# Attention segments turned by VectorE in 32x32 blocks, and the output projection as four 128x32 quarters

## The chip, the cores and the metric

The kernel runs on one core of a Trainium2 chip. A core has TensorE (matrix products into PSUM, an accumulator memory of eight banks of 512 fp32 columns on 128 partitions), VectorE, ScalarE, GpSimd (the Pool) and SyncE, which issues DMAs. The profile calls them PE, DVE, ACT, POOL and SP, and TensorE's loads of the stationary operand PEld. The metric is the device time of one execution in microseconds.

## The reference

Four layers run one after the other on a sequence of 2048 positions of 512 features, each added to its input after a layer normalisation without weights:

```python
# layers 0 and 2: 32 query heads of 16, one key head and one value head for all
q = (x @ wq) as 32 heads;  k = x @ wk;  v = x @ wv
p = softmax(q . k * 16 ** -0.5)            # 2048 x 2048 for each head
x = x + (p @ v, heads side by side) @ wo
# layers 1 and 3: linear attention with phi(t) = (t + 1 if t > 0 else exp(t)) + 1e-6
kv = phi(k)^T v for each head;  z = sum of phi(k)
x = x + (phi(q) kv / (phi(q) z + 1e-6)) @ wo2
```

The inputs are bf16. Nearly all the work is in the softmax of layers 0 and 2: 2 x 32 x 2048 x 2048 scores, each with an exponential.

## The kernel before, in words

**Tiles.** The sequence is cut into 16 tiles of 128 positions. The queries of a tile are stored as 128 partitions by 512 columns: partition 32 j + 16 r + d, column 128 g + position, for head (g, j, r) and feature d. One score block is the product of 128 keys with four heads of one query tile: rows 32 j to 32 j + 31 of the array, 512 columns. The keys are stored twice, each time with half of the 32 rows masked to zero (`KM`, `kmask`), so that parity r = 0 or 1 selects a head of the pair. Two layers have 2 x 16 tiles x 2 parities x 16 key tiles x 4 = 4096 blocks.

**Segments.** All blocks of one query tile and one parity make a segment (`Seg`), 64 blocks (64 segments in both layers together). The value products of a segment (`pv_try`, L1213) add into one PSUM bank, `ACC`: group j writes partitions 32 j to 32 j + 31, of which 16 are the output, one is the sum of the exponentials and the rest are zero. Four groups run side by side in the array. A few segments at the start of a layer (four in layer 0, eight in layer 2) are done in pieces, as keys become ready, and their pieces are added up in SBUF (`sg.unit`, L1523 and L1525).

**Who takes the exponentials.** Two sets of three banks take turns. TensorE fills a set in one round of score products (`qk`, L1159). ScalarE does two, sometimes three, of the blocks of a set with one instruction (L1350). VectorE may take the third (`dve_split`) or one in a spare bank (`dve_open`): it writes the bits of an approximate power of two as an int16 (L1454); GpSimd makes three shifted copies of it with integer adds (L1496), and the four are used with four weighted values. A block of ScalarE needs one value product, one of VectorE four. Which engine takes a block is decided while the program is built, by thresholds on VectorE's and the buffers' backlog.

**The order of work.** The program's order is planned ahead: `Planner` goes through the program in time with the durations written beside each operation, and gives every engine a fixed list. Smaller `prio` goes first; `Pool_` objects hand out banks and buffers. A mode is kept with each TensorE operation: `row` for scores, `col` for value products, `full` for the others; a change of mode costs time in the plan. `TABLE` sets thresholds of the planner (such as `BLS`, `BLT`, `SPX` on VectorE's backlog, `FBS`, `LOW` on free buffers, `HMAX`, `HTOL`, `STICK` on TensorE's order) by planned time in microseconds. During the attention stretches nearly all banks belong to the two sets; bank 7 serves everything else, projections and statistics of the neighbouring layers included.

**The end of a segment.** `norms` copies the accumulator to SBUF as fp32 (L1523). `norm` then turns it with four 128x128 fp32 products with an identity (L1610) into a bank, takes the reciprocal of the sums (L1620) and multiplies (L1624) into `Osb`, now positions by features. When both parities of a tile are there, `epilogue` transposes `Osb` into `OT`, by a DMA for tiles below 12 and by TensorE above, multiplies with `wo` in four 128x128x512 products (`mm`, L844), and adds to `x_sb` (L1664). The last tile of each attention layer has versions of its own that work in halves, so that one half runs while the other waits (`norm_halves`, `epi_crit`).

**Setup.** Masks and the bf16 identity are made on VectorE and the Pool from a ramp and its transpose before the first tile (L774 to L789), `wo` is loaded in eight DMAs (L753).

Of the kernel before, what the change touches and what calls it, by code (L numbers as in the profile page):

```python
# [11 lines left out]
ALU = mybir.AluOpType  # L12
# [24 lines left out]
class Planner:  # L37
# [50 lines left out]
    def op(self, opts, reads=(), writes=(), prio=5.0, lat=0.08, dma=False, name="", join=None, mode="full", port=False, after=(), over=()):  # L88

        if not self.calm and any(k[0] == "bank" and k[1] == 7 for k in list(writes) + list(reads) if type(k) is tuple):  # L90
# [4 lines left out]
            if PE in opts and prio > DPP and self.ws(("bank", 7)) and all(x.eng != PE or not x.done for x in self.ws(("bank", 7))) and mode == "full":  # L95
                prio = DPP + 0.001 * prio
# [324 lines left out]
class Seg:  # L421
# [11 lines left out]
    def take(self, js, back=False):  # L433
# [61 lines left out]
       2: ONE, 3: [[0, 1], [2, 3], [4, 5], [6, 7], [8, 9], [10, 11], [12, 13]] + ONE[14:]}  # L495
# [26 lines left out]
PVE = 0.6  # L522
PHP = 5.9
# [36 lines left out]
    (5, dict(EVP=2.2, FBS=8, HTOL=0.12)),  # L560
    (180, dict(BLS=2.3, DPP=1.0, EVP=2.2, FBS=8, HTOL=0.12)),
    (210, dict(BLS=2.3, DPP=1.0, EVP=2.2, FBS=8, HMAX=0.35, HTOL=0.12, LOW=10)),
    (630, dict(BLS=2.3, BLX=2.4, DPP=1.0, EVP=1.2, FBS=8, HMAX=0.35, HTOL=0.12, LOW=10, OWNP=1.0, STICK=1.5)),
    (660, dict(BLS=2.3, BLT=3.4, BLX=2.4, DPP=1.0, EVP=1.2, FBS=8, HMAX=0.1, HTOL=0.12, LOW=10, OWNP=1.0, SPX=1.5, STICK=1.5)),
    (690, dict()),
    (720, dict(BLT=2.9, BLX=1.25, CHT=19, LOW=10)),
    (750, dict(BLT=2.9, BLX=1.25, CHT=19, LOW=10, OWNP=1.0, SPX=1.5)),
]
BASE = dict(BLS=BLS, BLT=BLT, BLX=BLX, CHT=CHT, DPP=DPP, EVP=EVP, FBS=FBS, HMAX=HMAX, HTOL=HTOL, LOW=LOW, OWNP=OWNP, SPX=SPX, STICK=STICK)


def bass_interleave_layers__grouped_kv_mqa__linear_attn_block__prompt_kernel(
# [33 lines left out]
    WO = [("wo", c, gl) for c in range(4) for gl in range(2)]  # L606
# [15 lines left out]
    rampT = sb("rampT", [P, 32], FP32)  # L622
    eps1 = sb("eps1", [1, H], BF16)
# [105 lines left out]
    def B_(i):  # L729
        return ("bank", i)  # L730
# [16 lines left out]
    def late():  # L747
        yield ("flag", ("K", 0, T - 1))
        pool_op(lambda e: e.memset(va[:].rearrange("p t (h c) -> p (t h) c", c=17)[:, :, DH:DH + 1], 1.0), [("va", i) for i in range(8)], dur=1.2, prio=5.0)
        wov = A_wo.rearrange("(gh gl j r d) c -> r gh gl j d c", gh=2, gl=2, j=4, r=2)  # L750
        for c in range(4):
            for gl in range(2):
                dma(wo[64 * gl:64 * gl + 64, c, :], wov[c // 2, c % 2, gl], [("wo", c, gl)], 3.0, 3.5)  # L753
# [19 lines left out]
    pool_op(lambda e: e.memset(ident[:], 0.0), ["ident"])  # L773
# [6 lines left out]
    for j in range(4):  # L780
        q_ = slice(32 * j, 32 * j + 32)
        o = op({DV: (0.1, lambda e, q_=q_: e.tensor_tensor(out=ident[q_, q_], in0=ramp[q_, :], in1=rampT[q_, :], op=ALU.is_equal))},
               reads=["ramp", "rampT"], writes=["ident"], prio=-4.0, lat=0.12, join=o)
# [1383 lines left out]
```

## Time and profile before

| what | us |
|---|---|
| median of three runs | 1362.88 |
| lowest and highest | 1362.84, 1363.64 |
| the profiled execution | 1362.91 |
| its span, first to last instruction | 1361.2 |
| first and last exponential of the attention layers (L1350) start at | 11.4 and 1325.4 |

The span is 1.7 us shorter than the time of the same execution, which also holds what lies before the first and after the last instruction. A line of a group gives line of the source, engine, operation, tiles written and read, shapes and count, then after the bar the time in which at least one of them ran, the mean length of one in ns, and after the second bar the time that the engine stood idle before them, with what ended it. Records of one engine can overlap, so a count times the mean can exceed the busy time. A line of a timeline gives start and length in us, the engine, the line and how many instructions are merged.

### The profile page before, as it was taken

The page shows a single profiled execution, that of the slowest core. Times are in us where ns is not written, and L with a number is a line of the kernel's source. Part 1 is how long each engine was busy: PE and PEld are TensorE (multiplying, and loading weights), DVE is VectorE, ACT ScalarE, POOL GpSimd, SP SyncE. Part 2 cuts the span into 40 slices and gives each one's busy share as a digit, 9 for nine tenths or more (in the row PEclk, how much of TensorE's full clock was granted, in tenths as well). Part 3 has the DMA queues.
Part 4 walks back from the last instruction along what each step waited for, and adds up shares of the span by engine and source line. Part 5 has one row for each costly group of instructions (what it writes and reads, how often), then busy time and mean ns, then how long its engine had stood idle before and what let it go on. Part 6 is the DMA issues. An engine that isn't in the chain of part 4 may idle for free.

```text
span 1361.2 us, 38320 instructions
## 1 busy us (share of the span) xinstructions
PE 1316.0 (97%) x14984; PEld 460.5 (34%) x15067; DVE 1216.7 (89%) x2195; ACT 1328.3 (98%) x1536; POOL 1054.8 (77%) x1063
## 2 busy tenths in 40 slices
PE   8999999999999999999999999999999999999998
PEld 4322323223333223223743323333332323233235
DVE  8899898999989999997879998889998899998987
ACT  7999999999999999999799999999999999999996
POOL 1699798989989898987005897768898798988980
PEclk9999999999999999999999999999999999999999
DMA  4300000000000000000022000000000000000001
GB/s 106 98 6 13 6 9 9 6 13 2 13 6 14 5 6 6 2 2 2 2 43 44 9 6 17 13 6 6 13 3 13 6 13 6 6 6 2 2 2 63
DMA packets 52482, 20.59 MB, mean 15 GB/s; under 512 B 46160, under 2 KB 51792, under 8 KB 52304
## 3 DMA queue, kind: packets, MB, share of 16 engines
q1 hardware_dynamic: 51248, 18.10, 6.2%
q8 instruction: 122, 2.00, 0.6%
q14 instruction: 56, 0.46, 0.1%
q10 hardware_dynamic: 1056, 0.03, 0.0%
HBM read 5.28 MB, written 2.10 MB: 5 GB/s over the span
## 4 chain that ended last, share of the span: by engine, by line
PE 54%; ACT 30%; issue 8%; DVE 6%; POOL 2%; DMA 0%; SPq 0%; ACTq 0%; POOLq 0%; DVEq 0%
ACT W L1350 28%; PE ps L1213 22%; PE ps L1159 17%; PE ps L844 6%; PE ps L1038 3%; DVE W L1454 3%; POOL W L1496 2%; PE ps L1610 2%; PE ps L1260 2%; ACT phE L1694 1%; DVE sacc L1523 0%; DVE xn L767 0%; DMA W<-xn 0%; PE ps L897 0%; ACT ve L927 0%
## 5 line engine op out<-in xcount | busy, mean ns | idle before, releaser
L1350 ACT ACTIVATE W<-ps 128x1024 bf16<-128x1024 f32 (+1 forms) x1330 | 1273.2, 1146 | 2.4 <-PE ps L1159 2.1
L1496 POOL INT64_ADD W<-W x1023 | 1047.9, 1036 | 268.9 <-DVE W L1454 124.6
L1454 DVE TENSOR_SCALAR W<-ps 128x512 int16<-128x512 f32 x1362 | 889.7, 684 | 89.7 <-PE ps L1159 72.8
L1213 PE MATMUL ps<-W,VV 128*32 128x512 bf16 x8182 | 616.8, 384 | 4.2 <-DVE sacc L1523 3.5
L1159 PE MATMUL ps<-W,KM 32*128 32x512 bf16 x4096 | 520.5, 385 | 18.7 <-ACT W L1350 12.7
L1159 PEld LDWEIGHTS ps<-W,KM 32*128 32x128 bf16 x4096 | 130.1, 91 | 496.8 <-ACT W L1350 441.4
L1213 PEld LDWEIGHTS ps<-W,VV 128*32 128x32 bf16 x8182 | 148.9, 94 | 251.4 <-issue 162.2
L844 PE MATMUL ps<-wqkv,W 128*128 128x512 bf16 (+1 forms) x230 | 66.6, 368 | 7.5 <-issue 5.1
L1694 ACT ACTIVATE phE<-ps 128x512 bf16<-128x512 f32 (+1 forms) x66 | 44.6, 677 | 3.9 <-PE ps L1038 2.6
L1260 PE MATMUL ps<-W,V 128*32 128x512 bf16 (+4 forms) x173 | 46.4, 340 | 0.4 <-DVE KM L1026 0.3
L1610 PE MATMUL ps<-identF,sacc 128*128 128x128 f32 x240 | 41.8, 289 | 0.0
L1523 DVE COPY sacc<-ps 128x512 f32<-128x512 f32 x60 | 40.8, 680 | 1.0 <-PE ps L1213 0.8
L938 DVE BATCH_NORM_STATS2 st<-x_sb 128x6 f32<-128x512 bf16 x60 | 40.5, 680 | 0.3
L1038 PE MATMUL ps<-W,wqkv 128*128 128x128 bf16 x512 | 39.4, 220 | 0.3 <-DVE W L1701 0.3
L1038 PE MATMUL ps<-W,wq 128*128 128x128 bf16 x464 | 35.8, 220 | 0.0
L844 PE MATMUL ps<-wo,OT 128*128 128x512 bf16 x90 | 29.4, 383 | 4.8 <-issue 3.3
L1038 PEld LDWEIGHTS ps<-W,wqkv 128*128 128x128 bf16 x512 | 30.2, 98 | 9.0 <-issue 5.7
L767 DVE TENSOR_SCALAR phE<-phE 128x513 bf16<-128x513 bf16 x50 | 21.2, 424 | 13.4 <-ACT phE L1694 12.3
L1610 PEld LDWEIGHTS ps<-identF,sacc 128*128 128x128 f32 x240 | 25.5, 141 | 16.1 <-issue 10.6
L1038 PEld LDWEIGHTS ps<-W,wq 128*128 128x128 bf16 x464 | 26.3, 98 | 12.3 <-issue 9.2
L844 PEld LDWEIGHTS ps<-wqkv,W 128*128 128x128 bf16 x272 | 18.3, 97 | 30.6 <-issue 19.1
L767 DVE TENSOR_SCALAR xn<-x_sb,mv,rs 128x513 bf16<-128x513 bf16 x52 | 27.1, 530 | 0.3 <-ACT rs L929 0.2
(156 smaller groups left out, 550.0 us busy)
## 6 DMA issues: line engine op xcount, KB each, us to landing
out_dram<-x_sb SPq DMA_DIRECT2D x16, 128.0 KB, 1.7
x_sb<-in_A_x_dram SPq DMA_DIRECT2D x6, 256.0 KB, 4.7
wqkv<-in_B_wqkv_dram SPq DMA_DIRECT2D x1, 1536.0 KB, 8.8
W<-xn SPq DMA_TRANSPOSE x46, 2.5
x_sb<-in_A_x_dram SPq DMA_DIRECT2D x4, 128.0 KB
wq<-in_A_wq_dram SPq DMA_DIRECT2D x1, 512.0 KB
wo<-in_A_wo_dram SPq DMA_DIRECT2D x8, 64.0 KB
wo<-in_B_wo_dram SPq DMA_DIRECT2D x1, 512.0 KB, 9.7
```

The source lines that it names most:

```text
L767: return e.add_instruction(mybir.InstTensorScalarPtr(name=nc.get_next_instruction_name(), engine=mybir.EngineType.DVE, op0=op0, op1=op1, i ...
L844: return e.matmul(dst, lhsT=l, rhs=r, start=(k == 0), stop=(k == len(pairs) - 1))
L1038: ins = e.matmul(dst[:, g * P:(g + 1) * P], lhsT=lhs(g, k), rhs=rhs(k), start=(k == 0), stop=(k == FT - 1))
L1159: return e.matmul(bank(b), lhsT=KM[r, sg.par, kt * P:(kt + 1) * P], rhs=QT[r, sg.t, :], start=True, stop=True)
L1213: ins = e.matmul(ps[32 * j:32 * j + 32, ACC * 512:(ACC + 1) * 512], lhsT=VV[:, kt, 0 if w is None else 1 + w, :], rhs=ap, start=(k == 0), ...
L1260: o = op({PE: (n / 2400.0, lambda e: e.matmul(ps[32 * j:32 * j + 32, b * 512:b * 512 + n], lhsT=V0[:], rhs=QT[:, sg.t, 0:n], start=st, sto ...
L1350: ex = op({AC: (EXO + 0.4267 * n, lambda e, n=n, s_=s_, p_=p_: e.activation(ws_(p_), ps[:, s_ * 512:(s_ + n) * 512], ACTF.Exp, scale=EXPSC ...
L1454: o = op({DV: (0.602, lambda e: e.tensor_scalar(out=dst.bitcast(I16), in0=bank(b), scalar1=VB, scalar2=VLO, op0=ALU.add, op1=ALU.max))}, w ...
L1496: o = op({PO: (512 * m * PSR + PSO, lambda e, g_=g_, f_=f_: e.int64_add(ws_(g_).bitcast(I64), ws_(f_).bitcast(I64), step))}, reads=wk_(f_) ...
L1523: o = op({DV: (0.6, lambda e, src=src: e.tensor_copy(src, bank(ACC)))}, writes=[B_(ACC)] + key, prio=0.0, lat=0.15)
L1610: o = op({PE: (0.12, lambda e, c=c: e.transpose(ps[:, b * 512 + c * P:b * 512 + (c + 1) * P], src[:, c * P:(c + 1) * P], identF[:]))}, rea ...
L1694: op({AC: (0.07 + n / 1200.0, lambda e: e.activation(phE[:, i, 0:n], bank(b, n), ACTF.Exp))}, reads=[B_(b)], writes=[("phE", i)], prio=pr ...
```

## The change

The accumulator is no longer copied and turned by TensorE. VectorE reads it with its own transpose, which turns each 32x32 block in place within the 128x512 tile: what was at partition 32 j + i, column 128 c + 32 b + a comes to partition 32 j + a, column 128 c + 32 b + i. Positions are now split: the partition holds the head group j and the position's low five bits a, the columns hold the position's block b. Reciprocal and multiply follow from SBUF, with the reciprocals in a PSUM bank taken for that only. For segments done in pieces the transpose comes after the last addition, as an instruction of its own from SBUF to SBUF.

`Osb` gets columns in the order b, c, r, d, so that a 128x128 transpose of its block b gives c, r, d on partitions and j, a in columns. The output projection therefore sums over j, and for each j has four products of 128x32 (one for each b), each writing 32 partitions of the result: `quarters`, in the mode `col`. `wo` is loaded in the matching order in four DMAs. The versions in halves for the last tile go away: that tile takes the common way, then two half transposes and a projection in two halves of 256 columns, in quarters too.

In the setup the masks come from two comparisons, the identity from one comparison and one multiply after the first tile's mean, and the memsets for the shifted values stand later in the Pool's queue. In layer 2, the normalisation of tiles 8 to 15 goes in pairs. `TABLE` has new rows, 16 for 8, and sets two more parameters (`AHEAD`, `DXB`); a threshold on the priority of products into bank 7 now holds for the mode `col` as well.

```diff
+TRD = 0.625
+    def quarters(e, b, cs, l, r, start, stop):
+        ins = None
+        for q in range(4):
+            ins = e.matmul(ps[32 * q:32 * q + 32, b * 512 + cs.start:b * 512 + cs.stop], lhsT=l[:, q, :], rhs=r, start=start, stop=stop)
+        return ins
...
                 if sg.first and sg.last:
                     a_ = yield ("acq", as_pool, 0.0)
                     src, key = acc_(a_)
+                    o = op({DV: (TRD, lambda e, src=src: e.transpose(src, bank(ACC)))}, writes=[B_(ACC)] + key, prio=0.0, lat=0.15)
                 else:
                     a_, (src, key) = None, acc_(sg.unit)
-                if sg.t in ECRIT and sg.par:
...
-        def norm_halves(sg, src, key, a_):
...
-        def epi_crit(t, k, m, pr):
...
         def norm(sg, src, key, a_):
...
+            if a_ is None:
+                raw, was = src, key
+                yield from until(*was)
+                a_ = yield ("acq", as_pool, pr)
+                src, key = acc_(a_)
+                op({DV: (TRD, lambda e: e.transpose(src, raw))}, reads=was, writes=key, prio=pr, lat=0.15)
...
-            for c in range(4):
-                o = op({PE: (0.12, lambda e, c=c: e.transpose(ps[:, b * 512 + c * P:b * 512 + (c + 1) * P], src[:, c * P:(c + 1) * P], identF[:]))},
-                       reads=key + ["identF"], writes=[B_(b)], prio=pr, lat=0.2)
...
-            v4 = bank(b).rearrange("p (c j d) -> p c j d", c=4, j=4)
-            rr = rden[:, r_, :].rearrange("p (c j) -> p c j", j=4)
+            v4 = src.rearrange("p (c b q) -> p c b q", c=4, b=4)
+            rr = bank(b, 16).rearrange("p (c b) -> p c b", b=4)
...
-            dst = Osb[:, oslot[sg.t], 256 * sg.par:256 * sg.par + 256].rearrange("p (g j d) -> p g j d", g=4, j=4)
+            dst = Osb[:, oslot[sg.t], :].rearrange("p (b c r d) -> p r c b d", b=4, c=4, r=2)[:, sg.par]
...
             pl.give_after(banks, b, [o])
+            pl.give_after(as_pool, a_, [o])
...
+            lhs = lambda j: OT[:, m, :, 32 * j:32 * j + 32]
+            if t in ECRIT:
+                bs = yield from acq2(pr)
+                proj2(bs, lhs, lambda j, hs: wo[:, j, hs], t, [("OT", m)] + WO, pr, True)
...
-            o = mm(bank(b), [(OT[:, m, g, :], wo[:, g, :]) for g in range(4)], [("OT", m)] + WO, b, pr, 0.9)
+            for j in range(4):
+                o = op({PE: (0.222, lambda e, j=j: quarters(e, b, slice(0, 512), lhs(j), wo[:, j, :], j == 0, j == 3))},
+                       reads=[("OT", m)] + WO, writes=[B_(b)], prio=pr, lat=0.2, mode="col")
...
-        wov = A_wo.rearrange("(gh gl j r d) c -> r gh gl j d c", gh=2, gl=2, j=4, r=2)
-        for c in range(4):
-            for gl in range(2):
-                dma(wo[64 * gl:64 * gl + 64, c, :], wov[c // 2, c % 2, gl], [("wo", c, gl)], 3.0, 3.5)
+        wov = A_wo.rearrange("(g j q) c -> g q j c", g=4, j=4)
+        for g in range(4):
+            dma(wo[32 * g:32 * g + 32, :, :], wov[g], [("wo", g)], 3.0, 4.5)
...
-       2: ONE, 3: [[0, 1], [2, 3], [4, 5], [6, 7], [8, 9], [10, 11], [12, 13]] + ONE[14:]}
+       2: ONE[:8] + [[8, 9], [10, 11], [12, 13], [14, 15]], 3: [[0, 1], [2, 3], [4, 5], [6, 7], [8, 9], [10, 11], [12, 13]] + ONE[14:]}
...
+    def unit():
+        while not pl.ws(("mv", 0)):
+            yield ("sleep", 0.1)
+        yield from until(("mv", 0))
+        op({DV: (0.2, lambda e: e.tensor_tensor(out=ramp[:], in0=ramp[:], in1=rampT[:], op=ALU.is_equal))}, reads=["rampT"], writes=["ramp"], prio=-4.0, lat=0.05)
...
 TABLE = [
-    (5, dict(EVP=2.2, FBS=8, HTOL=0.12)),
...
-    (750, dict(BLT=2.9, BLX=1.25, CHT=19, LOW=10, OWNP=1.0, SPX=1.5)),
+    (5, dict(FBS=8, LOW=10)),
...
+    (150, dict(AHEAD=20, BLS=1.9, BLX=1.5, DPP=1.5, DXB=-1, FBS=22, LOW=10, OWNP=2.0, STICK=1.0)),
...
+    (750, dict(AHEAD=10, BLT=2.2, HMAX=0.35, HTOL=0.02)),
...
+    (1290, dict(BLS=2.3, BLX=1.0, EVP=0.95, HMAX=0.1, SPX=3.0, STICK=0.5)),
 ]
```

165 lines of the change are left out of this document (55 added, 110 removed).

## The prediction

> **What bounds it now.** I read the page's busy shares first, then the chain that ended last.
>
> ```profile
> span 1361.2 us, 38320 instructions
> ...
> PE 1316.0 (97%) x14984; PEld 460.5 (34%) x15067; DVE 1216.7 (89%) x2195; ACT 1328.3 (98%) x1536; POOL 1054.8 (77%) x1063
> ...
> PE 54%; ACT 30%; issue 8%; DVE 6%; POOL 2%; DMA 0%; SPq 0%; ACTq 0%; POOLq 0%; DVEq 0%
> ```
>
> TensorE and ScalarE are both full, and the chain swaps between them. Shares over the whole span hide the ends, so next I took the two long stretches in which an attention layer runs and the setup, layer change and tail are outside (columns: length, then busy us and count of PE, PEld, DVE, ACT, POOL), with one good 30 us window:
>
> ```profile
> 60.00:630.00 570.00, 555.65 (x6437) 173.86 (x6470) 524.11 (x900) 569.62 (x638) 517.51 (x507) 1.00 0.04 7
> 750.00:1320.00 570.00, 551.38 (x6407) 181.35 (x6441) 512.45 (x888) 570.00 (x638) 483.23 (x472) 1.00 0.04 8
> ```
> ```profile
> 90.00:120.00 30.00, 28.57 (x352) 8.51 (x350) 28.64 (x51) 30.00 (x34) 29.25 (x30) 1.00 0.03 6
> ```
>
> ScalarE has no hole at all. VectorE has: 45.9 us in the first stretch, 57.6 in the second, 103.5 together, about 9%; in the good window only 4.5%. So the time is the number of score blocks left to ScalarE times its pace. That pace is in its timeline:
>
> ```profile
> 444.53 7.48 ACT L1350 ACTIVATE W<-ps 128x1024 bf16<-128x1024 f32 x8
> 451.76 0.74 ACT L1694 ACTIVATE phE<-ps 128x512 bf16<-128x512 f32 x1
> 452.24 48.46 ACT L1350 ACTIVATE W<-ps 128x1024 bf16<-128x1024 f32 x52
> ```
> ```profile
> L1350 ACT ACTIVATE W<-ps 128x1024 bf16<-128x1024 f32 x1254 | 1178.7, 1123 | 1.1 <-PE ps L1159 0.9
> L1454 DVE TENSOR_SCALAR W<-ps 128x512 int16<-128x512 f32 x1362 | 889.7, 684 | 89.7 <-PE ps L1159 72.8 <-POOL W L1496 0.8
> L1496 POOL INT64_ADD W<-W x1023 | 1047.9, 1036 | 268.9 <-DVE W L1454 124.6 <-DVE mv L939 79.6 <-PE ps L1213 23.4
> L1213 PE MATMUL ps<-W,VV 128*32 128x512 bf16 x8182 | 616.8, 384 | 4.2 <-DVE sacc L1523 3.5 <-DVE W L1525 0.3
> ```
>
> Eight exponentials of two blocks start over 7.48 - 1.12 = 6.36 us, 0.908 each; the 52 over 47.34 us, 0.928 each. A block costs ScalarE about 0.454 us at its best pace. A block given to VectorE costs it 889.7 / 1362 = 0.653 us, the Pool 1047.9 / 1362 = 0.769 us, and TensorE three more value products than the one that a ScalarE block needs (2734 + 4 x 1362 = 8182, the count of L1213). That exchange, ScalarE against VectorE, is what the change can alter; 72.8 of VectorE's 89.7 us of waiting before L1454 are for a score product, so TensorE's order decides how much it gets.
>
> **The change, step by step.** First the fp32 transposes of each segment on TensorE, which go away. This is one, with the rounds beside it:
>
> ```profile
> 64.23 0.39 PE L1159 MATMUL ps<-W,KM 32*128 32x512 bf16 x3
> ...
> 64.55 0.66 PE L1610 MATMUL ps<-identF,sacc 128*128 128x128 f32 x4
> ...
> 65.14 0.39 PE L1159 MATMUL ps<-W,KM 32*128 32x512 bf16 x3
> 65.40 0.24 DVE L1620 RECIPROCAL rden<-ps 128x16 f32<-128x16 f32 x1
> ...
> 66.19 0.41 DVE L1624 TENSOR_TENSOR Osb<-ps,rden 128x256 bf16<-128x256 f32 x1
> ...
> 67.09 0.40 PE L1159 MATMUL ps<-W,KM 32*128 32x512 bf16 x4
> ...
> 67.42 0.62 PE L1213 MATMUL ps<-W,VV 128*32 128x512 bf16 x8
> ...
> 67.97 0.39 PE L1159 MATMUL ps<-W,KM 32*128 32x512 bf16 x3
> ```
> ```profile
> L1610 PE MATMUL ps<-identF,sacc 128*128 128x128 f32 x240 | 41.8, 289 | 0.0
> ...
> L1610 PE MATMUL ps<-identF,W 128*128 128x128 f32 x8 | 1.5, 294 | 0.0
> ```
>
> Four transposes fill the gap between two score rounds (64.23 to 65.14 = 0.91 us); the same gap (67.09 to 67.97 = 0.88 us) otherwise takes eight value products. There are 248 / 4 = 62 such groups, so 62 x 8 = 496 products find room, enough for 496 / 3 = 165 blocks moved to VectorE. TensorE is thus no longer the limit; VectorE is. Also the spare bank was held from 64.55 to 66.60 (2.05 us); it is now taken at the reciprocal, 65.40, so 0.85 us less, 53 us over 62 segments, for work that queues for that bank.
>
> Second, VectorE's side. The copy out of the accumulator becomes a transpose of the same 128x512 fp32 values:
>
> ```profile
> L1523 DVE COPY sacc<-ps 128x512 f32<-128x512 f32 x60 | 40.8, 680 | 1.0 <-PE ps L1213 0.8
> ```
> ```profile
> L778 DVE STREAM_TRANSPOSE rampT<-ramp x1: 211/211/211, 3.5 to 3.5; 128x32 f32<-128x32 f32 x1
> ```
>
> The trace has one transpose, 32 columns in 211 ns, and none of 512. Copies run at (680 - 420) / 256 = 1.0 ns a column (0.42 us is a 256-column copy, quoted with the tail below). From below: 211 + 480 x 1.0 = 0.69 us. From above: the copies' fixed part is 680 - 512 = about 0.17 us, so 32 columns cost 211 - 170 = 41 ns beyond it, 1.3 ns a column, and if the fixed part from SBUF is only 0.15, 1.9 ns: 0.15 + 512 x 1.9 = 1.12 us. I take 0.71, near the copy, because one extra fill of a 32-column block explains the 211. [...] Of the 64 segments 52 are transposed straight out of the accumulator: 52 x 0.03 = 1.6 us more. The other twelve, begun early (four in layer 0, eight in layer 2), keep their copy and adds and need a transpose beside them: 12 x 0.71 = 8.5 us. Reciprocal and multiply keep their shapes (0.24 and 0.41), with their operands' places swapped: nothing. VectorE's load grows by 10.1 us. The accumulator is released 0.03 us later, with the next segment's value products queued behind it; score rounds cover that, and bare it would be 1.6 us.
>
> Third, how much of VectorE's room is used. Each block moved costs VectorE 0.653 and shortens its own time by the 0.454 that ScalarE saves, so blocks = (room used - 10.1) / 1.107. All 103.5 us: 84 blocks, 38.3 us. None: the 10.1 us act against it, 10.1 / 1.107 x 0.454 = 4.1 us lost. I take half, 51.7: (51.7 - 10.1) / 1.107 = 37.6 blocks, **-17.1 us**. Half because the good window above shows 4.5% idle, which over 1140 us would be 51. The Pool needs 37.6 x 0.769 = 29 us of its 139 idle in the stretches. The new table of thresholds is the hand that moves the blocks; I cost it at nothing of its own, within 5 us either way: the two stretches run under different rows of the old table and differ by 524.1 - 512.5 = 11.6 us of VectorE work, 11.6 / 1.107 x 0.454 = 4.8.
>
> Fourth, the output projection in quarters: four products of 128x32 side by side for each of 128x128. The eight value products above are two such sets in 0.62 us, 0.24 a set after the first:
>
> ```profile
> 87.52 0.61 PE L844 MATMUL ps<-wo,OT 128*128 128x512 bf16 x2
> ```
>
> A full product takes 0.61 - 0.38 = 0.23. Equal, so 0. What could differ is the weight loads, sixteen small ones for four:
>
> ```profile
> 63.68 0.12 PEld L1213 LDWEIGHTS ps<-W,VV 128*32 128x32 bf16 x8 [0.23 <-issue]
> ```
> ```profile
> L1213 PEld LDWEIGHTS ps<-W,VV 128*32 128x32 bf16 x8182 | 148.9, 94 | 251.4 <-issue 162.2 <-POOL W L1496 22.6 <-DVE sacc L1523 10.3
> ...
> L844 PEld LDWEIGHTS ps<-wo,OT 128*128 128x128 bf16 x120 | 7.7, 97 | 14.8 <-issue 10.7 <-DVE W L1454 2.5 <-DVE W L1701 0.2
> ```
>
> Eight loads of a quarter lie within 0.12 us, so they overlap. One after the other and in the open, 16 x 0.094 - 4 x 0.097 = 1.1 us would come to each projection; that end goes to a rival. [...]
>
> Fifth, the last tile of an attention layer. It loses its version in halves:
>
> ```profile
> 1327.41 0.42 DVE L1517 COPY sacc<-ps 128x256 f32<-128x256 f32 x1 [2.00 <-PE ps L1213]
> ...
> 1330.04 0.39 PE L897 MATMUL ps<-wo,OT 128*128 128x256 bf16 x2
> ...
> 1330.36 0.76 DVE L910 BATCH_NORM_STATS2 st<-ps 128x6 f32<-128x256 f32 x2 [0.73 <-PE ps L897]
> ...
> 1331.99 0.41 DVE L952 TENSOR_SCALAR xn<-x_sb,mv,rs 128x512 bf16<-128x512 bf16 x1 [0.60 <-ACT rs L929]
> ...
> 1332.90 0.37 ACT L860 COPY W<-ps 128x256 bf16<-128x256 bf16 x1 [0.94 <-PE ps L873]
> ```
>
> Copy to statistics is 2.95 us. After: 0.71 + 0.24 + 0.41, then PE transposes as in 1332.40 to 1332.90 = 0.50, the copy 0.37, a wait 0.06, and four sets of 256 columns: three at 0.11 and the 0.32 from 1330.04 to 1330.36 = 0.65. Sum 2.94, with 0.15 of semaphores 3.1. Two layers at +0.2: **+0.4 us** (0 to 1.4, the latter with a dear transpose and open loads).
>
> Sixth, setup and statistics.
>
> ```profile
> 3.86 0.47 DVE L782 TENSOR_TENSOR ident<-ramp,rampT 32x32 bf16<-32x32 f32 x2
> ...
> 4.48 0.43 DVE L782 TENSOR_TENSOR ident<-ramp,rampT 32x32 bf16<-32x32 f32 x2
> ...
> 4.96 0.69 DVE L938 BATCH_NORM_STATS2 st<-x_sb 128x6 f32<-128x512 bf16 x1
> ...
> 6.58 0.41 DVE L952 TENSOR_SCALAR xn<-x_sb,mv,rs 128x512 bf16<-128x512 bf16 x1 [0.60 <-ACT rs L929]
> ```
>
> The 0.90 us of identity leaves the way of the first statistics and goes into the hole of 0.60 before L952. If x has landed: -0.9; if not: 0; I take **-0.5**. Were the hole missed, the transposes behind it would be late by some 0.5. Four fewer pairs of Ln and Exp in layer 2's normalisation (332 and 243 ns):
>
> ```profile
> L927 ACT ACTIVATE ve<-mv,eps 128x1 f32<-128x1 f32 x24 | 8.0, 332 | 2.7 <-DVE mv L939 2.7
> ...
> L929 ACT ACTIVATE rs<-ve 128x1 f32<-128x1 f32 x24 | 5.8, 243 | 0.2
> ```
>
> At most 2.3 us; records overlap, so half, **-1.2**. The projection's weights come in four DMAs for eight, on SP's queue behind the last keys' loads and far ahead of the first projection; the memsets for the shifted copies move behind the masks in the Pool's queue, ahead of the first score block that VectorE takes (after the keys of tile 7). Both 0; late, they would hold the first user for their own length, some 2 us.
>
> Sum: -17.1 + 0.4 - 0.5 - 1.2 = -18.4, span 1342.8. The profiled execution took 1362.91, 1.7 beside its span, and the median of the runs is 1362.88: 1344.5.
>
> **Rivals.** *TensorE was not what held VectorE back*: the freed gaps fill with idling and 10.1 us of VectorE work stay, 1362.9 + 4.1 - 1.3 (the ends and statistics) = 1365.7; or, if a tenth more of the hole closes (10.4 us), 1361.6. For it: VectorE's share is cut by thresholds on its own backlog, not TensorE's. Against: 72.8 us of its waiting are for score products.
>
> *All of VectorE's hole is used*: 1362.9 - 38.3 - 1.3 = 1323.3; three quarters of it (77.6 us), 61 blocks, 27.7 us, 1333.9. Against: the good window keeps 4.5%, and in it the Pool is at 29.25 of 30.
>
> *The transpose is dear* (the slower side): at 1.12 us VectorE gains 64 x 1.12 - 52 x 0.68 = 36.3 us of load, 36.3 / 1.107 x 0.454 = 14.9 us; where the hole isn't used, 1362.9 + 14.9 - 1.3 = 1376.5; where half is, 51.7 covers 36.3 and it comes to 1355. It decides once load exceeds the room gained: with a third of the hole used (34.5 us), from (34.5 + 35.4) / 64 = 1.09 us. For it: 211 ns at 32 columns is more than a copy's line gives. Against: one fill explains it.
>
> *The quarters' loads lie open*: 32 projections x 1.1 = 35 us take back what 62 groups at 65.14 - 64.55 = 0.59 us free, 37; TensorE stands as before and the 10.1 us of VectorE remain, 1366. The overlap of the value products' loads speaks against it.
>
> **How the numbers follow.** Forecast 0.54, its own range 1336 to 1354; the whole hole 0.17; TensorE not the limit 0.14; dear transpose 0.10; open loads 0.05. The range 1325 to 1364 holds the forecast's, most of the second and third, and leaves out the far ends. A measurement here tells about 0.2%, 2.7 us. Faster by more: 0.54 + 0.17, 0.03 of the third and 0.02 of the fourth, 0.76; within: 0.06 of the third and 0.02 of the last two, 0.08; slower: the rest, 0.16.
>
> **What would show it.** L1610 gone, no fp32 transposes of segments; STREAM_TRANSPOSE of 128x512 near 0.71 us, 64 of them; L1454's count near 1400; VectorE's idle time in the two stretches near 5%; ScalarE full at the same 0.91; quarters as sets within 0.24. A count of 1362 or less, or transposes over 1.0, would make the forecast wrong; so would more fillers in the old gaps.

## The result, and the profile after

| | median us | lowest to highest | runs |
|---|---|---|---|
| before | 1362.91 | 1362.84 to 1363.64 | 4 |
| changed | 1347.12 | 1346.89 to 1351.36 | 4 |

The ratio is 0.989, with a 95% interval of 0.9871 to 0.991: the changed kernel is 15.8 us faster. Its profiled execution took 1346.96 us. Some executions had a granted clock of 0.994 to 0.997 in place of 1.0, with which the same kernel took 2 to 6 us longer: here the one of 1351.36 us, below three of ten of the changed kernel with the first shifts and one of ten with the second, two of four of the old kernel with the second shifts, two of four with the quarters one after another, and all four with load on VectorE. The page of the changed kernel, with span, busy shares and the chain that ended last:

```profile
span 1345.2 us, 39031 instructions
...
PE 1301.1 (97%) x15334; PEld 436.1 (32%) x15391; DVE 1225.8 (91%) x2224; ACT 1314.6 (98%) x1523; POOL 1077.2 (80%) x1085
...
PE 49%; ACT 30%; issue 9%; DVE 8%; POOL 2%; DMA 1%; ACTq 0%; POOLq 0%; DVEq 0%
```

TensorE's share of the chain fell from 54% to 49%, VectorE's rose from 6% to 8%. ScalarE is as full as it was. The two long stretches of the changed kernel (columns as in the prediction; the last exponential now starts at 1309.3, so the second holds ten us of the tail, which that of the kernel before does not):

```profile
60.00:630.00 570.00, 556.66 (x6672) 165.16 (x6699) 533.47 (x927) 569.76 (x641) 533.61 (x524) 1.00 0.04 7
750.00:1320.00 570.00, 553.21 (x6708) 177.39 (x6728) 520.70 (x918) 564.64 (x643) 493.95 (x482) 1.00 0.04 8
```

VectorE's idle time in them is 36.5 and 49.3 us, 85.8 together, for 103.5 before. With the second stretch cut at 1300 us, where neither kernel is in its tail, it is 76.6 for 102.3, 6.8% of 1120 us. The view of one line gives shortest, median and longest duration in ns and the first and last start; the shapes behind them are those of a sample. Here are the exponentials of ScalarE, in the changed kernel over the whole span and from 640 us on, then in the kernel before from 650 us on:

```profile
L1376 ACT ACTIVATE W<-ps x1322: 1003/1152/1702, 9.5 to 1309.3; 128x1024 bf16<-128x1024 f32 x182, 128x1536 bf16<-128x1536 f32 x7
...
L1376 ACT ACTIVATE W<-ps x669: 1012/1148/1690, 657.8 to 1309.3; 128x1024 bf16<-128x1024 f32 x157, 128x1536 bf16<-128x1536 f32 x11
```
```profile
L1350 ACT ACTIVATE W<-ps x671: 1017/1157/1654, 668.5 to 1325.4; 128x1024 bf16<-128x1024 f32 x160, 128x1536 bf16<-128x1536 f32 x8
```

With 11.4 us for the first exponential before, the 16.0 us of span divide so:

| part | before | after | difference |
|---|---|---|---|
| start to the first exponential | 11.4 | 9.5 | -1.9 |
| from there to layer 2's first (layers 0 and 1) | 657.1 | 648.3 | -8.8 |
| layer 2's first to its last | 656.9 | 651.5 | -5.4 |
| from there to the end | 35.8 | 35.9 | +0.1 |

The groups of the changed kernel that answer to the prediction's steps, and one group of the kernel before that was not shown:

```profile
L1480 DVE TENSOR_SCALAR W<-ps 128x512 int16<-128x512 f32 x1394 | 902.8, 682 | 65.9 <-PE ps L1185 54.7 <-POOL W L1522 0.2
L1522 POOL INT64_ADD W<-W x1047 | 1070.1, 1036 | 228.2 <-DVE W L1480 174.0 <-PE ps L1239 12.0 <-PE ps L861 5.6
L1239 PE MATMUL ps<-W,VV 128*32 128x512 bf16 x8278 | 631.3, 384 | 3.6 <-DVE sacc L1540 2.4 <-DVE sacc L1544 0.7 <-DVE sacc L1546 0.4
L904 PE MATMUL ps<-wo,OT 128*32 128x512 bf16 x480 | 38.4, 385 | 0.4 <-DVE W L855 0.4
L1540 DVE STREAM_TRANSPOSE sacc<-ps 128x512 f32<-128x512 f32 x52 | 36.8, 707 | 10.1 <-PE ps L1239 10.1
L1567 DVE STREAM_TRANSPOSE sacc<-sacc 128x512 f32<-128x512 f32 x10 | 7.0, 700 | 0.0
...
L1286 PE MATMUL ps<-W,V 128*32 128x512 bf16 (+5 forms) x229 | 61.1, 336 | 1.2 <-DVE W L1666 0.3
```
```profile
L1260 PE MATMUL ps<-W,V 128*32 128x512 bf16 (+4 forms) x173 | 46.4, 340 | 0.4 <-DVE KM L1026 0.3
```

VectorE takes 1394 blocks for 1362, 32 more, and 32 x 0.454 = 14.5 us answers to the 14.2 that the two middle rows of the table gave up. The value products rose by 96 = 3 x 32. L1286 (L1260 before) are fillers, products with zero weights that the planner puts where TensorE would otherwise stand still: they grew too, from 46.4 to 61.1 us, all of it in the two long stretches (26.0 to 40.9 us, the second up to 1310). TensorE's fp32 transposes took 44.8 us (41.8 and 1.5 of L1610, and 1.5 in the version in halves). Of that, 14.5 went to value products (616.8 to 631.3) and 14.7 to fillers. What became of the rest can't be read from TensorE's busy time as a whole, 1316.0 and 1301.1: the traces hold fewer products than loads, 83 fewer before (14984 to 15067) and 57 after, so some products were not recorded.

### The profile page after: what moved, and what is told of

It is laid out like the page before. It is cut to its first block, busy times and chain, and to the rows that moved or that the text cites. A ratio compares the mean times of both kernels' runs of the same rounds, so it can differ in the third digit from the quotient of the medians.

```text
span 1345.2 us, 39031 instructions
## 1 busy us (share of the span) xinstructions
PE 1301.1 (97%) x15334; PEld 436.1 (32%) x15391; DVE 1225.8 (91%) x2224; ACT 1314.6 (98%) x1523; POOL 1077.2 (80%) x1085
## 4 chain that ended last, share of the span: by engine, by line
PE 49%; ACT 30%; issue 9%; DVE 8%; POOL 2%; DMA 1%; ACTq 0%; POOLq 0%; DVEq 0%
ACT W L1376 29%; PE ps L1239 20%; PE ps L1185 16%; PE ps L861 5%; DVE W L1480 4%; PE ps L1064 3%; POOL W L1522 2%; PE ps L904 2%; PE ps L1286 1%; ACT phE L1659 1%; PE ps L1170 1%; DVE sacc L1540 1%; DVE sacc L1666 0%; DVE xn L776 0%; DMA W<-xn 0%
## 5 line engine op out<-in xcount | busy, mean ns | idle before, releaser
L1376 ACT ACTIVATE W<-ps 128x1024 bf16<-128x1024 f32 (+1 forms) x1322 | 1257.4, 1157 | 1.7 <-PE ps L1185 1.5
L1522 POOL INT64_ADD W<-W x1047 | 1070.1, 1036 | 228.2 <-DVE W L1480 174.0
L1480 DVE TENSOR_SCALAR W<-ps 128x512 int16<-128x512 f32 x1394 | 902.8, 682 | 65.9 <-PE ps L1185 54.7
L1239 PE MATMUL ps<-W,VV 128*32 128x512 bf16 x8278 | 631.3, 384 | 3.6 <-DVE sacc L1540 2.4
L1185 PE MATMUL ps<-W,KM 32*128 32x512 bf16 x4096 | 517.6, 385 | 22.2 <-ACT W L1376 12.9
L1286 PE MATMUL ps<-W,V 128*32 128x512 bf16 (+5 forms) x229 | 61.1, 336 | 1.2 <-DVE W L1666 0.3
L1540 DVE STREAM_TRANSPOSE sacc<-ps 128x512 f32<-128x512 f32 x52 | 36.8, 707 | 10.1 <-PE ps L1239 10.1
L904 PE MATMUL ps<-wo,OT 128*32 128x512 bf16 (+1 forms) x544 | 40.5, 372 | 0.4 <-DVE W L855 0.4
L1064 PEld LDWEIGHTS ps<-W,wqkv 128*128 128x128 bf16 x512 | 29.9, 98 | 10.3 <-issue 7.8
L776 DVE TENSOR_SCALAR phE<-phE 128x513 bf16<-128x513 bf16 x50 | 21.1, 422 | 10.1 <-ACT phE L1659 8.9
L1579 DVE TENSOR_TENSOR Osb<-sacc,ps 128x256 bf16<-128x256 f32 x64 | 26.0, 407 | 0.4
L1286 PEld LDWEIGHTS ps<-W,V 128*32 128x32 bf16 x229 | 18.2, 95 | 24.5 <-issue 10.6
```

Of the source, the lines that this page charges most:

```text
L776: return e.add_instruction(mybir.InstTensorScalarPtr(name=nc.get_next_instruction_name(), engine=mybir.EngineType.DVE, op0=op0, op1=op1, i ...
L904: ins = e.matmul(ps[32 * q:32 * q + 32, b * 512 + cs.start:b * 512 + cs.stop], lhsT=l[:, q, :], rhs=r, start=start, stop=stop)
L1064: ins = e.matmul(dst[:, g * P:(g + 1) * P], lhsT=lhs(g, k), rhs=rhs(k), start=(k == 0), stop=(k == FT - 1))
L1185: return e.matmul(bank(b), lhsT=KM[r, sg.par, kt * P:(kt + 1) * P], rhs=QT[r, sg.t, :], start=True, stop=True)
L1239: ins = e.matmul(ps[32 * j:32 * j + 32, ACC * 512:(ACC + 1) * 512], lhsT=VV[:, kt, 0 if w is None else 1 + w, :], rhs=ap, start=(k == 0), ...
L1286: o = op({PE: (n / 2400.0, lambda e: e.matmul(ps[32 * j:32 * j + 32, b * 512:b * 512 + n], lhsT=V0[:], rhs=QT[:, sg.t, 0:n], start=st, sto ...
```

## The experiments

The theory after the result: time on TensorE, freed from the fp32 transposes, let VectorE take 32 blocks more, and each is worth ScalarE's 0.454 us. Against it stand three rivals: that the new table, a better fitted plan, did it alone; that TensorE had room anyway; and that VectorE alone is now the limit, as the prediction had it. Every kernel below computes the whole result.

**Table and structure apart.** One kernel is the changed one with the old rows, the other the old one with the new rows.

```diff
 # old_table: the changed kernel with the old rows
-    (5, dict(FBS=8, LOW=10)),
...
-    (1290, dict(BLS=2.3, BLX=1.0, EVP=0.95, HMAX=0.1, SPX=3.0, STICK=0.5)),
+    (5, dict(EVP=2.2, FBS=8, HTOL=0.12)),
...
+    (750, dict(BLT=2.9, BLX=1.25, CHT=19, LOW=10, OWNP=1.0, SPX=1.5)),
 # new_table: the same edit the other way round, on the kernel before
```

> The changed kernel with the table of thresholds of the kernel before; all else as changed. Theory 1 (the work taken off TensorE is what moves blocks to VectorE, the table only adjusts to it): most of the 16 us stays, 1347 to 1355 us, and L1480 counts more than 1362 blocks. Theory 2 (the gain is the new table's, the transposes on VectorE bring nothing of their own): 1362.9 us or more, 1362 blocks or fewer.

> The kernel before with the table of the changed kernel; all else as before. Theory 1: no gain, 1362.9 us or slower, because TensorE still has the four fp32 transposes of each segment, and the table is not fitted to that. Theory 2: the gain comes along, about 1347 us.

The blocks that VectorE took, in the groups of the changed kernel with the old table and of the old kernel with the new one:

```profile
L1472 DVE TENSOR_SCALAR W<-ps 128x512 int16<-128x512 f32 x1382 | 899.1, 683 | 73.9 <-PE ps L1177 61.5 <-POOL W L1514 0.8
```
```profile
L1462 DVE TENSOR_SCALAR W<-ps 128x512 int16<-128x512 f32 x1350 | 882.6, 685 | 97.4 <-PE ps L1167 82.6 <-POOL W L1504 0.4
```

| structure | table | median us | ratio to before (95%) | blocks |
|---|---|---|---|---|
| changed | old | 1352.66 | 0.9919 (0.9902 to 0.9935) | 1382 |
| before | new | 1375.87 | 1.0089 (1.0074 to 1.0104) | 1350 |

With the old table the change still gains 11.0 us (the kernel before took 1363.69 beside it); the new table on the old structure costs 12.2. So the table alone is not the cause. But a table that doesn't belong to its structure cost 5.5 us here and 12.2 there, so part of any comparison is fit.

**How much of a time is fit?** To learn that, nine or eleven of the durations that the planner works with are moved by 1 to 3 ns. That changes nothing in the program but what the planner makes of it: the order, and which engine takes a block. Each set of shifts is applied to both kernels.

```diff
 # jit_new and jit_old
-QK_DUR = 0.22
+QK_DUR = 0.221
-QK_LAT = 0.438
+QK_LAT = 0.435
 # likewise EXO .0645, EX_LAT .188, DH_DUR .221, AH_DUR .281, LAGP .053, DTL 3.602, PSO .169
 # jit_new_b and jit_old_b: QK_DUR .222, SWITCH .108, PV_LAT .213, EXO .0645, EX_LAT .187,
 # DH_DUR .219, AH_DUR .278, LAG .182, LAGP .047, DTB 4.598, PSO .171
```

> The changed kernel, with nine of the durations that its planner assumes moved by 1 to 3 ns; the work is the same, the planned order differs. Theory 1 in its plain form (the time follows from the engines' loads): within 3 us of 1347.1. Theory 3 (the time depends on how well table and plan fit each other, and a plan that is not picked is worse by several us): 1350 to 1365 us, and the same loss for the kernel before with the same shifts, so that 16 us between the two remain.

> The kernel before with the same shifts of 1 to 3 ns in the same nine planned durations. Theory 1 plain: within 3 us of 1362.9. Theory 3: 1365 to 1380 us, about 16 us above the changed kernel with these shifts.

> The changed kernel with a second set of shifts: ten planned durations moved by 1 to 3 ns. The first set gave 1357.9 us (changed) against 1370.7 (before). Theory 3 (a fixed advantage of the structure, and on top of it a fit of table and plan that any shift loses): 1353 to 1366 us here, and 10 to 20 us below the kernel before with the same shifts. If the advantage were itself an accident of the fit, the difference would have no fixed sign.

> The kernel before with the second set of shifts. Theory 3: 1368 to 1382 us, 10 to 20 us above the changed kernel with the same shifts.

The same group in the four, in this order:

```profile
L1480 DVE TENSOR_SCALAR W<-ps 128x512 int16<-128x512 f32 x1371 | 891.1, 683 | 82.3 <-PE ps L1185 66.5 <-POOL W L1522 3.8
```
```profile
L1454 DVE TENSOR_SCALAR W<-ps 128x512 int16<-128x512 f32 x1354 | 884.7, 685 | 93.9 <-PE ps L1159 76.4 <-POOL W L1496 0.4
```
```profile
L1480 DVE TENSOR_SCALAR W<-ps 128x512 int16<-128x512 f32 x1367 | 887.8, 682 | 82.9 <-PE ps L1185 70.6 <-POOL W L1522 0.3
```
```profile
L1454 DVE TENSOR_SCALAR W<-ps 128x512 int16<-128x512 f32 x1348 | 879.2, 685 | 93.8 <-PE ps L1159 78.6 <-POOL W L1496 0.4
```

| durations | before | changed | difference |
|---|---|---|---|
| as given | 1362.91 | 1347.12 | -15.8 |
| first set | 1370.73 | 1357.86 | -12.9 |
| second set | 1379.95 | 1360.33 | -19.6 |

The shifts made all four slower: the old structure by some 7.0 and 16.6 us (each against the kernel before on its own chip), the changed one by 10.7 and 13.2. So by these two sets both kernels as given are orders that came out well. The difference between the structures kept its sign in every pair, 12.9 to 19.6 us, with 17 and 19 blocks between them. The structure's part is thus shown; its size is known to some 4 us either way, from three pairs. How much of it the blocks explain differs: 14.5 of the 15.8 us as given, but 17 x 0.454 = 7.7 of 12.9 and 19 x 0.454 = 8.6 of 19.6 in the shifted pairs. What makes up the rest there was not found.

**Load put back on one engine, in the same order.** In the next two kernels the planned durations stay, so every engine's list is the changed kernel's, with more work in it. Eight fp32 products with the identity come ahead of each projection of 30 tiles, or a second transpose ahead of each of the 52 that read the accumulator.

```diff
 # pe_load
+            def work(e, j):
+                if j == 0:
+                    for c in range(8):
+                        e.transpose(ps[:, b * 512 + c % 4 * P:b * 512 + (c % 4 + 1) * P], identF[:], identF[:])
+                return quarters(e, b, slice(0, 512), lhs(j), wo[:, j, :], j == 0, j == 3)
...
-                o = op({PE: (0.222, lambda e, j=j: quarters(e, b, slice(0, 512), lhs(j), wo[:, j, :], j == 0, j == 3))},
...
+                o = op({PE: (0.222, lambda e, j=j: work(e, j))},
...
 # dve_load
-                    o = op({DV: (TRD, lambda e, src=src: e.transpose(src, bank(ACC)))}, writes=[B_(ACC)] + key, prio=0.0, lat=0.15)
+                    o = op({DV: (TRD, lambda e, src=src: (e.transpose(idle[:], bank(ACC)), e.transpose(src, bank(ACC)))[1])}, writes=[B_(ACC)] + key, prio=0.0, lat=0.15)
```

> The changed kernel in its own order, with eight fp32 128x128 transposes of the identity put ahead of each of the 30 output projections into the bank that the projection then starts anew: 240, about as many as the kernel before had, but the order does not know of them and nothing waits for them but TensorE. By 0.11 us each it is 26 us of TensorE's time plus a change of mode for each. Theory 1 (TensorE has no room in the rounds): nearly all of it shows, +20 to +35 us. Rival (TensorE's fillers and waits, 61 us of fillers, swallow it): under +8 us.

> The changed kernel in its own order, with a second transpose of the accumulator into an unused tile ahead of each of the 52 direct ones, 0.707 us each: 37 us of VectorE's time that the order does not know of, and the accumulator is released that much later. By my exchange price (load / 1.107 x 0.454, which holds for a plan that moves blocks away) 15 us; in a fixed order no block can move away, so where VectorE is the bound up to +37 us, and where it has its idle 7.5% for it, under +10.

The added groups and the lines that wait, of the kernel with load on TensorE, then of that with load on VectorE, then of the changed kernel (the last line of the second and of the third is from the view of waits: us in total, times, longest):

```profile
L1627 PE MATMUL ps<-identF 128*128 128x128 f32 x240 | 32.8, 280 | 0.4 <-DVE W L855 0.4
...
L1480 DVE TENSOR_SCALAR W<-ps 128x512 int16<-128x512 f32 x1394 | 902.1, 681 | 94.2 <-PE ps L1185 83.9 <-POOL W L1522 0.4
...
L1376 ACT ACTIVATE W<-ps 128x1024 bf16<-128x1024 f32 x1264 | 1185.6, 1105 | 23.3 <-PE ps L1185 22.9
```
```profile
L1541 DVE STREAM_TRANSPOSE idle<-ps 128x512 f32<-128x512 f32 x52 | 36.7, 706 | 10.0 <-PE ps L1240 10.0
L1541 DVE STREAM_TRANSPOSE sacc<-ps 128x512 f32<-128x512 f32 x52 | 35.0, 672 | 0.0
...
L1377 ACT ACTIVATE W<-ps 128x1024 bf16<-128x1024 f32 x1264 | 1189.7, 1092 | 13.4 <-PE ps L1186 11.5
...
PEld ps L1240 <- DVE sacc L1541: 23.1, 38, 1.5
```
```profile
L1376 ACT ACTIVATE W<-ps 128x1024 bf16<-128x1024 f32 x1264 | 1183.9, 1140 | 1.4 <-PE ps L1185 1.3
...
PEld ps L1239 <- DVE sacc L1540: 5.8, 13, 0.9
```

32.8 us on TensorE took the time to 1374.24 (ratio 1.0081, 1.0065 to 1.0096): the span grew by 27.4, 0.83 for each us put in, VectorE's wait for score products from 54.7 to 83.9, and that of ScalarE, the full engine, ahead of its exponentials of two blocks from 1.4 to 23.3. So TensorE had no room at these places of the order. 36.7 us on VectorE took it to 1371.88 (1.0062, 1.0047 to 1.0077), 24.9 of span, at most 0.7 for each; here the value products wait 23.1 us for the accumulator where they waited 5.8, and ScalarE 13.4 in place of 1.4. That VectorE alone is the limit falls with the first, that TensorE alone is with the second. But a fixed order can't answer a load by giving blocks to another engine, so these are prices of the order, not of the engines.

**The same load, planned anew.** So in the next two the planner knows of the load.

```diff
 # pe_back, in norm, once its bank is there
+            for c in range(4):
+                op({PE: (0.12, lambda e, c=c: e.transpose(ps[:, b * 512 + c * P:b * 512 + (c + 1) * P], src[:, c * P:(c + 1) * P], identF[:]))},
+                   reads=key + ["identF"], writes=[B_(b)], prio=pr, lat=0.2)
 # dve_twice, at the same place
+            op({DV: (TRD, lambda e: e.transpose(bank(b), src))}, reads=key, writes=[B_(b)], prio=pr, lat=0.15)
```

> The changed kernel, its order planned anew with four fp32 products with the identity put back on TensorE for every segment (248 of them, about 42 us busy as in the kernel before), into the bank that holds the reciprocals; their results are overwritten, the output is unchanged. VectorE's own transposes stay. If room on TensorE is what let VectorE take more blocks, the count falls from 1394 towards 1362 or below and the time goes to some 1360 to 1368 (the time before plus part of the 4 us of VectorE load). If TensorE had room, the time stays within the spread that small shifts of the plan gave, 1347 to 1360. A spread of 8 to 13 us for a table that no longer fits is contained in either, so only a time above 1360 or a count below 1367 (the lowest count of the shifted plans of the changed kernel) speaks clearly for the first.

> The changed kernel, its order planned anew with a second transpose of each segment on VectorE (62 more of about 0.70 us, 43 us), its result overwritten, the output unchanged. If VectorE is the limit after the change, 43 us of load move 43 / 1.107 = 39 blocks to ScalarE, 39 x 0.454 = 17.8 us: about 1365 with the table still fitting, count about 1355. If the 86 us that VectorE idles in the two stretches take it, the time stays within the spread of the shifted plans, 1347 to 1360. If both engines limit, this and the run with TensorE's transposes put back cost about alike.

The groups, then the two long stretches, of the kernel with TensorE's transposes put back:

```profile
L1480 DVE TENSOR_SCALAR W<-ps 128x512 int16<-128x512 f32 x1335 | 870.2, 683 | 91.8 <-PE ps L1185 77.9 <-POOL W L1522 0.2
...
L1574 PE MATMUL ps<-identF,sacc 128*128 128x128 f32 x256 | 46.8, 291 | 0.1
```
```profile
60.00:630.00 570.00, 554.65 (x6571) 172.93 (x6590) 516.64 (x892) 569.84 (x632) 508.93 (x497) 1.00 0.04 7
750.00:1320.00 570.00, 552.25 (x6517) 182.54 (x6539) 500.22 (x868) 569.17 (x627) 466.12 (x454) 1.00 0.04 8
```

And of the kernel with a second transpose on VectorE:

```profile
L1480 DVE TENSOR_SCALAR W<-ps 128x512 int16<-128x512 f32 x1359 | 884.2, 681 | 63.2 <-PE ps L1185 52.3 <-POOL W L1522 0.2
...
L1573 DVE STREAM_TRANSPOSE ps<-sacc 128x512 f32<-128x512 f32 x64 | 45.5, 711 | 0.5 <-PE ps L1286 0.4
```
```profile
60.00:630.00 570.00, 555.65 (x6595) 166.76 (x6614) 538.21 (x936) 569.81 (x638) 518.99 (x508) 1.00 0.04 7
750.00:1320.00 570.00, 552.18 (x6543) 174.45 (x6564) 530.28 (x927) 568.63 (x638) 481.10 (x469) 1.00 0.04 8
```

| load put back | busy us | median us | ratio to before (95%) | blocks | VectorE idle in the stretches |
|---|---|---|---|---|---|
| none | | 1347.12 | 0.989 (0.9871 to 0.991) | 1394 | 85.8 |
| TensorE | 46.8 | 1378.96 | 1.0117 (1.01 to 1.0134) | 1335 | 123.1 |
| VectorE | 45.5 | 1367.46 | 1.0031 (1.0019 to 1.0043) | 1359 | 71.5 |

TensorE's transposes back alone cost 31.8 us: 59 blocks return to ScalarE (59 x 0.454 = 26.8), and VectorE, with less to do, idles more than in the changed kernel: 121.3 us for 76.6 with the second stretch cut at 1300 us (70.2 with the second transpose on VectorE). That is the prediction's exchange, run backwards, above the 1360 to 1368 us expected and larger than the 16 us of the change; a loss of fit of some 11 to 13 us, as the shifts gave, may be in it and was not measured for this one. Time and count both lie beyond what the shifts did to the changed kernel (at most 13.2 us, and no fewer than 1367 blocks). The bank of the reciprocals is held longer here too, which this run doesn't tell apart. The second transpose on VectorE costs 20.3 us and 35 blocks, near the 17.8 us and 39 blocks expected of a limiting VectorE. A us on TensorE costs 0.68, one on VectorE 0.45. Both cost more than either set of shifts did, so both engines limit the changed kernel; that TensorE does so the more is likely and not shown, since the two times lie 11.5 us apart, no more than fit alone moved them.

**The quarters one after another.** The changed kernel in the same order, with the sixteen quarter products of a projection sorted by the quarter that they write, not by the head group that they sum over, so that four in a row write the same 32 partitions.

```diff
-            for j in range(4):
-                o = op({PE: (0.222, lambda e, j=j: quarters(e, b, slice(0, 512), lhs(j), wo[:, j, :], j == 0, j == 3))},
+            def column(e, q):
+                ins = None
+                for j in range(4):
+                    ins = e.matmul(ps[32 * q:32 * q + 32, b * 512:b * 512 + 512], lhsT=OT[:, m, q, 32 * j:32 * j + 32], rhs=wo[:, j, :], start=j == 0, stop=j == 3)
+                return ins
+            for q in range(4):
+                o = op({PE: (0.222, lambda e, q=q: column(e, q))},
```

> The changed kernel in its own order, with the sixteen 128x32 products of each of the 30 output projections sorted by quarter and not by j, so that four products in a row write the same 32 partitions. If the quarters run side by side only across different quarters, a projection takes 16 x 0.21 = 3.4 us for 0.9, 75 us of TensorE in all, and the time grows by 40 to 75 us. If the array overlaps them anyway, or they were never side by side, no change (within 2 us).

The projection's group in it and the first half of one projection, the first half of one in the changed kernel, and the group and one projection with full products in the kernel before with the first set of shifts (its trace holds all 120 products; the one of the kernel before as given holds 90):

```profile
L1627 PE MATMUL ps<-wo,OT 128*32 128x512 bf16 x480 | 71.2, 382 | 0.4 <-DVE W L855 0.4
...
112.42 1.05 PE L1627 MATMUL ps<-wo,OT 128*32 128x512 bf16 x8
```
```profile
112.67 0.61 PE L904 MATMUL ps<-wo,OT 128*32 128x512 bf16 x8
```
```profile
L844 PE MATMUL ps<-wo,OT 128*128 128x512 bf16 x120 | 35.8, 384 | 0.1
...
155.34 1.04 PE L844 MATMUL ps<-wo,OT 128*128 128x512 bf16 x4
```

The products' busy time grew from 38.4 to 71.2 us, the median to 1377.78 (ratio 1.0106, 1.0088 to 1.0123), 28.3 of span by the profiled execution, less than the 40 to 75 expected. So it is the interleaving of the four quarters that makes the projection cheap: 38.4 / 30 = 1.28 us for sixteen quarter products, against 35.8 / 30 = 1.19 for the four full ones.

**The setup undone.** The changed kernel with the masks, the identity and the Pool's memsets of the kernel before.

```diff
-    pool_op(lambda e: e.memset(quad[:], 0.0), ["quad"], dur=0.95, prio=-3.0)
+    pool_op(lambda e: e.memset(ident[:], 0.0), ["ident"])
...
+        o = op({DV: (0.1, lambda e, q_=q_: e.tensor_tensor(out=ident[q_, q_], in0=ramp[q_, :], in1=rampT[q_, :], op=ALU.is_equal))},
...
+    pool_op(lambda e: e.memset(VV[:, :, 1:NSH + 1, DH:32], 0.0), [("VP", t) for t in range(T)], dur=1.2, prio=1.55)
...
-        pool_op(lambda e: e.memset(VV[:, :, 1:NSH + 1, DH:32], 0.0), [("VP", t) for t in range(T)], dur=1.2, prio=2.6)
```

> The changed kernel with the masks, the identity and the memsets of the setup as before. By the traces the first exponential started at 11.4 us before and 9.5 after. If the setup alone does that, it starts at 11.2 to 11.6 here and the time grows by about 2 us, give or take what the different order of the rest brings; if the table or the order does it, it stays at 9.5.

The median is 1348.83 (ratio 0.9895, 0.9879 to 0.9912), 1.7 above the changed kernel, and the first exponential starts at 11.5 again. The start of the timeline, in the changed kernel and in this one:

```profile
1.70 0.17 DVE L785 TENSOR_SCALAR ramp<-ramp 128x4 f32<-128x4 f32 x1
...
3.14 0.69 DVE L964 BATCH_NORM_STATS2 st<-x_sb 128x6 f32<-128x512 bf16 x1
...
6.14 0.94 POOL L836 MEMSET VV<- 128x1024 bf16 x1
```
```profile
1.77 1.07 DVE L785 TENSOR_SCALAR ramp<-ramp 128x4 f32<-128x4 f32 x1
...
1.87 0.95 POOL L810 MEMSET VV<- 128x1024 bf16 x1
...
4.99 0.69 DVE L956 BATCH_NORM_STATS2 st<-x_sb 128x6 f32<-128x512 bf16 x1
```

The statistics start at 4.99 in place of 3.14. 0.90 us of that is one step of the ramp, 1.07 us beside the Pool's memset and 0.17 without it. Of the 2.0 us at the start, only 1.0 reaches the span: an earlier start is in part given back later (layer 2's first exponential comes at 659.2 for 657.8, its last at 1310.4 for 1309.3).

## Why the prediction was right, and where not

**The mechanism held.** 1347.12 was measured where 1344.5 was forecast, by the exchange that step three names: blocks moved to VectorE, three value products for each, 0.454 us each. In the kernels as given it accounts for nearly all of the gain; in the shifted pairs it accounts for about half. That their room came from the fp32 transposes is shown by putting them back (59 blocks, 31.8 us), and not only argued from their gaps. The signs to look for came in: L1610 gone, a count near 1400 (1394), ScalarE full. Two did not: VectorE's idle time is 85.8 us in the stretches, 7.5% (6.8% without the tail), not near 5%; and there are more fillers, which the prediction had named as evidence against itself. Both say the same: the freed room was used less than assumed.

**Step one, the room.** 165 blocks' worth of value products was counted as room, and from that "TensorE is thus no longer the limit; VectorE is". That is the step that failed: TensorE still limits, since 46.8 us put back on it cost 31.8, and VectorE doesn't limit alone. TensorE's 40.9 us of fillers in the stretches and VectorE's idle time there would fit if each lay at times when the other one isn't ready; no run shows that. The bank, freed earlier, was not tried alone.

**Step two, the transpose.** 0.707 us from the accumulator and 0.700 from SBUF, where 0.71 was taken between 0.69 and 1.12. From 211 ns at 32 columns to 700 at 512, both from SBUF to SBUF, it is (700 - 211) / 480 = 1.02 ns a column. A step of one fp32 column in SBUF took 153 ns in the kernel before, so 32 columns more at the copies' 1.0 ns would fit both lengths, 153 + 64 = 217 and 153 + 544 = 697 ns; that they are the fill of a block, as the prediction has it, no run shows. All of the expected 64 came: 62 in the two groups above, two more of 0.700 out of a borrowed buffer. Reciprocal and multiply cost nothing, as said: 249 and 407 ns, for 247 and 417 before. The later release of the accumulator is no cost: the value products wait 5.8 us for it and waited 10.3 before.

```profile
PEld ps L1213 <- DVE sacc L1523: 10.3, 26, 1.1
```

**Step three, how much of it is used, is the term that was mis-sized.** Half of the 103.5 us was taken, 37.6 blocks and 17.1 us; it was 32 blocks, and 14.5 by that price. In the formula, 32 x 1.107 + 10.1 = 45.5 us were used, 44%. The half came from one good window of the old trace, and no reason stood behind it but that; the runs give none for 44 either. The formula's own price was too high as well: by it VectorE's busy time would rise by 32 x 0.653 + 10.1 = 31.0 us, and it rose by 9.1 (1216.7 to 1225.8), the blocks' share by 13.1 (889.7 to 902.8), 0.41 each. So VectorE's idle time over the whole span fell by 25.1 us, not 45.5. The table, "at nothing of its own, within 5 us either way", was sized too narrow: 5.5 us between the two tables on the changed structure, 12.2 on the old one, and 7 to 17 for shifts of a few ns. The forecast's nearness is therefore partly luck, for another order of the same structure came out at 1357.86 and 1360.33, which lies in the range given but outside the forecast's own.

**Step four, the quarters.** Nearly nothing, as said: 1.28 us a projection against 1.19, 2.6 us of TensorE in all. The open loads, at 1.1 us a projection, fall as a rival; what would have cost is the order of the products, 2.37 us a projection one quarter after another, which the prediction didn't price.

**Step five, the last tile.** Copy to statistics was costed at 3.1 us where it was 2.95. In layer 2 of the changed kernel it is 1314.58 - 1311.40 = 3.18:

```profile
1311.40 0.72 DVE L1540 STREAM_TRANSPOSE sacc<-ps 128x512 f32<-128x512 f32 x1 [3.48 <-PE ps L1239]
...
1314.58 0.87 DVE L936 BATCH_NORM_STATS2 st<-ps 128x6 f32<-128x256 f32 x2
```

**Step six, setup and statistics.** The setup gave 1.9 us at the first exponential, not 0.5, beyond the bound of 0.9. The prediction looked at the identity's 0.90 us, which did leave the way, and passed over the ramp ahead of it, where a step of 1.07 us stood in the old trace beside the memset that the change moves. Undone alone, the setup is worth 1.0 us of span and 1.7 of the median. The statistics were costed at -1.2 by the count of pairs. The groups of the changed kernel, and the two of the kernel before that were not shown:

```profile
L953 ACT ACTIVATE ve<-mv,eps 128x2 f32<-128x2 f32 x20 | 8.3, 417 | 0.0
...
L955 ACT ACTIVATE rs<-ve 128x2 f32<-128x2 f32 x20 | 6.5, 327 | 0.0
L953 ACT ACTIVATE ve<-mv,eps 128x1 f32<-128x1 f32 x16 | 5.1, 321 | 1.6 <-DVE mv L965 1.5
L955 ACT ACTIVATE rs<-ve 128x1 f32<-128x1 f32 x16 | 3.7, 229 | 0.2
```
```profile
L927 ACT ACTIVATE ve<-mv,eps 128x2 f32<-128x2 f32 x16 | 5.8, 364 | 0.0
L929 ACT ACTIVATE rs<-ve 128x2 f32<-128x2 f32 x16 | 4.4, 275 | 0.0
```

Together 23.6 us for 24.0 before: 0.4 less, since those of two columns became longer (417 ns for 364). The gain was too small to see.

**The rivals.** "TensorE was not what held VectorE back" fell with the loads put back. "All of VectorE's hole is used" did not come: 85.8 us are left. The dear transpose and the open loads fell by their durations.

## What to carry to other kernels

Time freed on one of two engines that share a stretch need not all become work: of 44.8 us freed on TensorE here, 14.5 went to value products and 14.7 to fillers. So count what moved (blocks, value products, fillers), and price the change by that, not by the time freed. Where a planner makes the order, one run of one order says little about a structure: shifts of 1 to 3 ns in planned durations cost 7 to 17 us here, as much as the change gained, so compare structures over several orders of each. A change in the setup should be read from every long instruction at the start (here a step of 1.07 us that became 0.17), and from what stood beside it on the other engines.

## What the runs showed of the hardware

- A VectorE operation of four fp32 columns in SBUF took 1.07 us while a memset of 0.95 us ran on the Pool, in the kernel before and with the setup undone, and 0.17 us in the changed kernel, where that memset runs at 6.14. With the setup undone the step ended at 2.84 and the memset at 2.82, in the kernel before at 2.84 and 2.81; that the step waited for the memset fits these times; by what, no run shows. Beside the memset at 6.14 a VectorE aggregate took 0.17 us, the mean of its kind (170 ns).
- Sixteen products of 128x32 sorted by the quarter that they write cost 71.2 / 30 = 2.37 us a projection, interleaved over the four quarters 1.28. Eight of them, four in a row for each of two quarters, took 1.05 us, as long as four products of 128x128 (1.04), and eight interleaved took 0.61. The times fit that products to the same 32 partitions took turns, while in this order two quarters still ran beside each other.
- A second transpose of the same accumulator right behind the first took 672 ns, the first 706.
